# Splitting a two-layer product: full squares of the first two chunks on ScalarE, high and low matmuls in groups, later range checks, a third room for sums

## Chip, cores and metric

One NeuronCore of a Trainium2 chip. The metric is the device time of one execution, in microseconds; lower is better. The kernel before took 662.72 us (median of 3 runs, 662.3 to 664.31).

## What is computed

Attention with four sink columns and a window of 128, followed by two dense layers with a squared ReLU between them:

```python
keep = is_sink | in_window                      # 4 batches, 8 heads, 768 rows, 64 columns a head
a = softmax(where(keep, q @ k.T / 8, -1e9))
x = (a @ v), heads side by side                 # 3072 x 512
h = maximum(x @ w_in, 0)                        # 512 -> 2048
out = (h * h) @ w_out                           # 2048 -> 512
```

All of it is float32, and the result must be near float32.

## The kernel before

**Tiling.** The 3072 rows are eight chunks `c` of 384 (`TOK`). The 2048 hidden columns are 16 blocks `fc` of 128; one block of one chunk is called a column here, so there are 128 columns. The attention of a chunk (four pairs of heads) has to be done before its first column.

**A column.** Every operand is split into a high part (float32r, 4 bytes) and two float16 parts, the rounded high part and the rest. A product is then three matmuls: high by high, and two low ones with float16 weights. `first` (L1024) makes a column's hidden block: for each of four slices `cc` of the 512 inputs one high and two low matmuls, 12 in all, 384 columns wide, into one PSUM bank. The slices alternate, high-low-low and low-low-high. Then ScalarE makes `r`, the scaled ReLU (L1037), and its square `gh`, rounded to float32r (L1042). VectorE makes the square again at full precision in the bank (L1049) and subtracts `gh` from it (L1061), which is the low part `gc`; a cast (L511, L514) makes the float16 copy of `gh`. One column later `second` (L1084) multiplies these by the block of `w_out`: three groups `t` of 128 rows, each one high and two low matmuls, 512 wide, alternating in the same way, summed over all 16 blocks in three banks.

**Legs.** The columns are run in nine legs: the first 8 blocks of chunk 0, all 16 of chunk 1, the last 8 of chunk 0, then chunks 2 to 7. While the first two chunks run, the 32 rows of weights are still being loaded and split: ScalarE makes the high part (L427), VectorE puts the words together (L392, L399, L406) and makes the rest (L432). The attention of chunk 2 also lies there. `evacuate` (L1112) copies the three sums out at the end of a leg, into rooms `ob0`, `ob1` and, from chunk 2 on, `f2`; in the second leg of chunk 0 it first loads the part sums back.

**Range checks.** `scale_steps` (L479, 16 reductions of the split weights) are handed out with the columns of leg 3, which is chunk 2. `check_steps` and `value_steps` follow from leg 4. `verdict` (L1217) reduces all tables to a flag in one block of VectorE instructions six columns before the end.

**Order.** Nothing is scheduled at run time. `Plan` (L90) holds all steps with an engine or several, a cost, a rank, what they read and write, and which bank they take. `order` (L137) simulates the engines with these costs and writes each engine's instructions out in the order it finds: of the steps that can start soonest it takes the lowest rank, and a step with several engines goes to the one that ends first, plus a penalty in the fourth place. So a changed cost or choice moves instructions of all engines, far from the line that was changed.

Of the kernel before, what the change touches and what calls it, by code (L numbers as in the profile page):

```python
# [8 lines left out]
F32 = mybir.dt.float32  # L9
# [15 lines left out]
TOK = 384  # L25
NQ = TOK // P
WR = 512
BIG = 3.0e38
LIM = 5.0e8
W_LOW = 2.0**-22  # L30
W_HIGH = 2.0**33
# [29 lines left out]
TURNED = 2  # L61
# [3 lines left out]
CHECK = 4  # L65
# [3 lines left out]
G16_DVE = 0.2  # L69

# [135 lines left out]
def sink_window_attention_moe(  # L206
# [25 lines left out]
    with ExitStack() as fast:  # L232
# [139 lines left out]
        def bank(key):  # L372
            return banks[plan.got[key]]
# [631 lines left out]
        def products(c, f0, f1, item, checks):  # L1005
            xh, xc = xs[slot[c]]
            last = c == NCHUNK - 1
            pend = None
            for fc in range(f0, f1 + 1):
                n = item + fc - f0  # L1010
                if fc < f1:
# [5 lines left out]
                    for cc in range(NCC):  # L1017

                        def first(cc=cc, fc=fc, key=key):
                            wh, wc = wi[fc]()  # L1020
                            cols = slice(cc * P, (cc + 1) * P)
                            terms = ((wh, xh[:, cc]), (wc[:, 1], xc[:, 0, cc]), (wc[:, 0], xc[:, 1, cc]))
                            for j, (wt, xt) in enumerate(terms[:: -1 if cc % 2 else 1]):
                                nc.tensor.matmul(  # L1024
                                    bank(key)[:, 0:TOK], wt[:, cols], xt,
                                    start=(cc == 0 and j == 0), stop=(cc == NCC - 1 and j == 2),
                                )

                        add(
                            ("PE", 0.5, 0), n + 0.1 * cc, first,  # L1030
                            reads=[(t, slot[c], cc) for t in ("xh", "x16", "xl")] + [(t, 2 * fc) for t in ("w", "w16", "wl")]
                            + [(key, cc - 1)] * (cc > 0),
                            writes=[(key, cc)] + [("tick", n), "column"] * (cc == 0), take=[("h", key)] if cc == 0 else [],
                        )
# [3 lines left out]
                        reads=[(key, cc) for cc in range(NCC)], writes=["r"],  # L1038
# [13 lines left out]
                        reads=["r"], writes=[(key, cc) for cc in range(NCC)],  # L1052
# [16 lines left out]
                if pend:  # L1069
                    f, g, gh, gc = pend  # L1070
                    for t in range(NQ):
# [33 lines left out]

        def scaled(e, dst, src):
            if e == "ACT":
                nc.scalar.activation(dst, src, AF.Copy, scale=SUM_SCALE)
            else:
                nc.vector.tensor_scalar(dst, src, SUM_SCALE, None, op0=ALU.mult)  # L1110

        def evacuate(c, f0, f1, t, okey, n):  # L1112
# [3 lines left out]
            third = c >= 2  # L1116
# [100 lines left out]
        def verdict():  # L1217
            t = const.tile([P, 16], F32, name="checks")

            par = made["par"] = const.tile([P, 2], F32, name="par")  # L1220
# [5 lines left out]
            flat = vmax.rearrange("p a b -> p (a b)")  # L1226
            for x, (table, limit) in enumerate(
                (
                    (most[:, NCHUNK : NCHUNK + 2], LIM),
                    (wchk[:, 0, :], W_HIGH),  # L1230
                    (wchk[:, 1, :], 0.0),
                    (wmax, WS_MAX),
                    (flat, V_MAX),
                )
            ):
                at = x if x < 3 else x + 5
                nc.vector.tensor_reduce(t[:, at : at + 1], table, axis=AX.X, op=ALU.max)
                nc.vector.tensor_scalar(t[:, at : at + 1], t[:, at : at + 1], limit, None, op0=ALU.is_le)
            for at, table, limit in ((10, wmax, WS_MIN), (11, flat, V_MIN)):
                nc.vector.tensor_reduce(t[:, at : at + 1], table, axis=AX.X, op=ALU.min)  # L1240
                nc.vector.tensor_scalar(t[:, at : at + 1], t[:, at : at + 1], limit, None, op0=ALU.is_ge)
# [4 lines left out]
            made["good"] = const.tile([P, 1], F32, name="good")  # L1246
            nc.vector.tensor_reduce(made["good"], t[:, 0:12], axis=AX.X, op=ALU.min)
            made["ones"] = const.tile([P, 1], F32, name="ones")
            nc.vector.memset(made["ones"], 1.0)

# [10 lines left out]
        add(  # L1261
            ("DVE", 4.0), END, verdict,
            reads=["wchk", "wmax", "vmax", ("most", NCHUNK), ("most", NCHUNK + 1)],
            writes=["good"],
        )
# [242 lines left out]
```

## Time and profile before

| | |
|---|---|
| median of 3 runs | 662.72 us |
| the profiled execution | 662.91 us |
| its span, first to last instruction | 661.1 us |
| PE busy (matmul) | 643.0 us, 97% of the span |
| DVE, ACT, POOL busy | 485.2, 441.8, 183.3 us |
| mean granted TensorE clock | 0.996 |

PE is TensorE's matmul queue, PEld its weight loads, DVE VectorE, ACT ScalarE, POOL GpSimd. Matmuls overlap, so the start of one row may lie before the end of the row ahead of it; the distance from end to end is what a matmul costs in a dense stream. A busy PE is therefore not yet a PE at its peak.

### The profile page before, as it was taken

The page shows a single profiled execution, that of the slowest core. Times are in us where ns is not written, and L with a number is a line of the kernel's source. Part 1 is how long each engine was busy: PE and PEld are TensorE (multiplying, and loading weights), DVE is VectorE, ACT ScalarE, POOL GpSimd, SP SyncE. Part 2 cuts the span into 40 slices and gives each one's busy share as a digit, 9 for nine tenths or more (in the row PEclk, how much of TensorE's full clock was granted, in tenths as well). Part 3 has the DMA queues.
Part 4 walks back from the last instruction along what each step waited for, and adds up shares of the span by engine and source line. Part 5 has one row for each costly group of instructions (what it writes and reads, how often), then busy time and mean ns, then how long its engine had stood idle before and what let it go on. Part 6 is the DMA issues. An engine that isn't in the chain of part 4 may idle for free.

```text
span 661.1 us, 12158 instructions
## 1 busy us (share of the span) xinstructions
PE 643.0 (97%) x3734; PEld 405.8 (61%) x3734; DVE 485.2 (73%) x1328; ACT 441.8 (67%) x1358; POOL 183.3 (28%) x381
## 2 busy tenths in 40 slices
PE   8899999996999999999999999999999999999995
PEld 6665666663566566666666666666666665556663
DVE  8999999999778888776877867575767664343432
ACT  7998777765465565565578777777777785655421
POOL 4433414435223333332423122242322211000000
PEclk9999999998999999999999999999999999999999
DMA  8635554784745534455777767657667754322001
GB/s 289 246 128 182 168 196 122 219 239 115 198 136 165 156 109 128 126 165 152 182 200 213 218 202 193 174 166 202 173 175 220 219 173 141 124 88 72 17 1 53
DMA packets 85748, 106.54 MB, mean 161 GB/s; under 512 B 12760, under 2 KB 60376, under 8 KB 85676
## 3 DMA queue, kind: packets, MB, share of 16 engines
q1 hardware_dynamic: 85068, 105.05, 54.7%
q8 instruction: 31, 0.51, 0.3%
q10 hardware_dynamic: 576, 0.60, 0.3%
q14 instruction: 41, 0.34, 0.2%
q0 software_dynamic: 32, 0.05, 0.0%
HBM read 80.29 MB, written 24.38 MB: 158 GB/s over the span
## 4 chain that ended last, share of the span: by engine, by line
PE 88%; DVE 6%; DMA 2%; ACT 2%; issue 1%; POOL 0%; SPq 0%; DVEq 0%; ACTq 0%
PE bank L1024 37%; PE bank L1084 37%; PE bank L941 5%; PE bank L668 5%; PE bank L662 1%; DVE P L718 1%; PE bank L947 1%; DVE P L645 1%; DMA out_dram<-ob 1%; ACT P L651 1%; DMA sk<-SKT 1%; DVE wc L432 0%; DVE f L406 0%; DMA qn<-in_q_dram 0%; DVE f L399 0%
## 5 line engine op out<-in xcount | busy, mean ns | idle before, releaser
L1024 PE MATMUL bank<-xc,wc 128*128 128x384 f16 x1024 | 217.5, 329 | 0.5 <-DVE wc L432 0.5
L1084 PE MATMUL bank<-wc,gc 128*128 128x512 f16 (+1 forms) x800 | 215.1, 376 | 0.9 <-POOL gc L514 0.7
L1024 PE MATMUL bank<-xh,wh 128*128 128x384 f32 x512 | 198.8, 428 | 1.1 <-DVE gc L1061 0.6
L1084 PE MATMUL bank<-wh,gh 128*128 128x512 f32 (+1 forms) x400 | 166.9, 457 | 2.2 <-ACT gh L1042 1.6
L1037 ACT ACTIVATE r<-bank 128x384 f32<-128x384 f32 x128 | 62.6, 489 | 117.9 <-PE bank L1024 112.3
L1049 DVE SCALAR_TENSOR_TENSOR bank<-bank,r 128x384 f32<-128x384 f32 x128 | 72.0, 563 | 86.6 <-ACT r L1037 85.6
L718 POOL TENSOR_SCALAR P<-P,small 128x260 f32<-128x260 f32 (+1 forms) x164 | 87.1, 545 | 158.4 <-DVE small L711 150.5
L651 ACT ACTIVATE P<-P,nbs 128x260 f32<-128x260 f32 (+1 forms) x192 | 93.4, 487 | 43.8 <-DVE nbs L645 41.6
L1024 PEld LDWEIGHTS <-wc 128*128 128x128 f16 x1024 | 77.1, 98 | 70.0 <-issue 31.1
L1024 PEld LDWEIGHTS bank<-xh,wh 128*128 128x128 f32 x512 | 93.8, 190 | 25.6 <-DVE nbs L645 0.9
L1084 PEld LDWEIGHTS <-gc 128*128 128x128 f16 x800 | 56.1, 98 | 86.4 <-issue 48.8
L1084 PEld LDWEIGHTS bank<-wh,gh 128*128 128x128 f32 x400 | 76.2, 190 | 22.4 <-ACT gh L1042 2.1
L645 DVE CUSTOM_DVE_ANT_0 P<-bank,maskA 128x260 f32<-128x260 f32 x128 | 52.7, 420 | 30.7 <-PE bank L668 30.0
L668 PE MATMUL bank<-KS,QS 128*128 128x260 f32 (+1 forms) x288 | 69.0, 325 | 3.2 <-DVE nbs L645 2.4
L1061 DVE TENSOR_TENSOR gc<-bank,gh 128x384 f16<-128x384 f32 x128 | 70.1, 548 | 0.4
L1042 ACT ACTIVATE gh<-r 128x384 fp32r<-128x384 f32 x128 | 66.6, 520 | 3.0
L668 PEld LDWEIGHTS bank<-KS,QS 128*128 128x128 f32 x288 | 52.2, 190 | 14.3 <-DVE nbs L645 2.7
L877 DVE STREAM_TRANSPOSE T<-P 128x384 f32<-128x384 f32 x96 | 46.7, 495 | 1.0 <-POOL P L718 0.9
L625 POOL TENSOR_TENSOR KS<-kn,KS 128x396 fp32r<-128x396 f32 (+1 forms) x20 | 25.9, 1297 | 68.2 <-ACT KS L511 34.2
L941 PE MATMUL bank<-PT,vn 128*64 128x256 f32 (+1 forms) x392 | 37.0, 338 | 0.4 <-DVE xc L962 0.4
L651 ACT ACTIVATION_READ_ACCUMULATOR P<-P,nbs 128x1 f32 x192 | 36.0, 187 | 0.0
L511 DVE CAST gc<-gh 128x384 f16<-128x384 f32 x74 | 27.6, 373 | 10.4 <-ACT gh L1042 7.5
(129 smaller groups left out, 748.8 us busy)
## 6 DMA issues: line engine op xcount, KB each, us to landing
raw<-in_moe_w_dram SPq DMA_DIRECT2D x32, 512.0 KB, 3.7
half<-in_moe_w_dram SPq DMA_DIRECT2D x64, 256.0 KB, 2.9
via<-T SPq DMA_DIRECT2D x96, 96.0 KB, 2.0
PT<-via SPq DMA_DIRECT2D x24, 384.0 KB, 3.8
via<-T SPq DMA_DIRECT2D x96, 80.0 KB, 2.1
PT<-via SPq DMA_DIRECT2D x24, 320.0 KB, 3.9
kn<-in_k_dram SPq DMA_DIRECT2D x28, 264.0 KB, 4.3
qn<-in_q_dram SPq DMA_DIRECT2D x31, 192.0 KB, 3.6
```

The source lines that it names most:

```text
L645: nc.vector.tensor_tensor_reduce(Pt(h)[:, i, o : o + n], ps_[:, 0:n], mask[:, 0:n], -SCALE, BIG, ALU.add, ALU.min, nb)
L651: nc.scalar.activation(Pt(h)[:, i, o : o + n], Pt(h)[:, i, o : o + n], AF.Exp, bias=nb, scale=-1.0, accum_out=sm[:, h, i : i + 1],)
L668: nc.tensor.matmul(bank(key)[:, 0:n], QS(h)[:, cols], flat[:, a, c0 : c0 + n], start=(a == 0), stop=(a == 1),)
L718: {"POOL": nc.gpsimd, "DVE": nc.vector}[engine].tensor_scalar(a, a, rs[:, h, i : i + 1], 1.0, op0=ALU.mult, op1=ALU.mult)
L877: nc.vector.transpose(dst.rearrange("p c j b -> p j c b"), src.rearrange("p j (c b) -> p j c b", b=32))
L941: nc.tensor.matmul(xo[h * D : h * D + D, qs[0] * P : qs[0] * P + len(qs) * P], vn[:, kk, h, :], rhs(), start=(n == 0), stop=False, skip_gr ...
L1024: nc.tensor.matmul(bank(key)[:, 0:TOK], wt[:, cols], xt, start=(cc == 0 and j == 0), stop=(cc == NCC - 1 and j == 2),)
L1037: lambda key=key, r=r: nc.scalar.activation(r(), bank(key)[:, 0:TOK], AF.Relu, scale=R_SCALE),
L1042: lambda gh=gh, r=r, fc=fc: nc.scalar.activation(gh(), r(), AF.Square, accum_out=gsum[:, c % 2, fc : fc + 1]),
L1049: lambda key=key, r=r: nc.vector.scalar_tensor_tensor(bank(key)[:, 0:TOK], bank(key)[:, 0:TOK], R_SCALE, r(), op0=ALU.mult, op1=ALU.mult),
L1061: lambda key=key, gh=gh, gc=gc: nc.vector.tensor_tensor(gc()[:, 1], bank(key)[:, 0:TOK], f32(gh()), op=ALU.subtract),
L1084: nc.tensor.matmul(bank(okey)[:, cols], gt, wt[:, cols], start=(f == f0 and j == 0), stop=(f == f1 - 1 and j == 2),)
```

## The change

Four things are done:

1. The full square may go to ScalarE (`full_square`, as Square of `r` into the bank) or to VectorE. In the first two chunks VectorE carries a penalty of 3.0 us in the choice, from chunk 2 on none is set.
2. From chunk 2 on (`together`) a column's `first` is two steps: all 8 low matmuls, then all 4 high ones. In chunks 2 to 6, for the blocks but the last, `second` is two steps: the 3 high ones of all three sums, then the 6 low ones; the three banks are taken at once.
3. The weight reductions move from leg 3 to the last leg but one (chunk 6). The verdict is cut into small steps and starts a column earlier.
4. The second leg of chunk 0 uses the third room as well.

```diff
-                    for cc in range(NCC):
-                        def first(cc=cc, fc=fc, key=key):
...
+                    every = tuple(range(NCC))
+                    low_first = [(cc, x) for cc in every for x in (2, 1)]
+                    if together:
+                        runs = [low_first, [(cc, 0) for cc in every]]
+                    else:
+                        runs = [[(cc, x) for x in ((2, 1, 0) if cc % 2 else (0, 1, 2))] for cc in every]
+                    for m, run in enumerate(runs):
+                        def first(m=m, run=run, fc=fc, key=key, runs=runs):
+                            wh, wc = wi[fc]()
+                            for j, (cc, x) in enumerate(run):
...
-                        ("DVE", 0.47), n - 9,
-                        lambda key=key, r=r: nc.vector.scalar_tensor_tensor(
-                            bank(key)[:, 0:TOK], bank(key)[:, 0:TOK], R_SCALE, r(), op0=ALU.mult, op1=ALU.mult
-                        ),
+                        [("DVE", 0.47, "", 0.0 if together else FULL_DVE), ("ACT", 0.45)], n - 9,
+                        lambda e, key=key, r=r: full_square(e, bank(key)[:, 0:TOK], r()),
...
+                    if together and not last and f < f1 - 1:
+                        okeys = [("o", c, f0, t) for t in range(NQ)]
+                        def second_of(x, f=f, gh=gh, gc=gc, okeys=okeys):
+                            wh, wc = wo[f]()
+                            for t, okey in enumerate(okeys):
+                                ts_ = slice(t * P, (t + 1) * P)
+                                terms = ((gh()[:, ts_], wh), (gc()[:, 0, ts_], wc[:, 1]), (gc()[:, 1, ts_], wc[:, 0]))
+                                for j, (gt, wt) in enumerate(terms[1:] if x else terms[:1]):
...
+        def full_square(e, full, r):
+            if e == "ACT":
+                nc.scalar.activation(full, r, AF.Square)
+            else:
+                nc.vector.scalar_tensor_tensor(full, full, R_SCALE, r, op0=ALU.mult, op1=ALU.mult)
...
-            third = c >= 2
+            third = c >= TURNED or f0 > 0
...
-            for fc in range(f0, f1) if g == CHECK - 1 else ():
-                own[fc] = [scales.pop(0)]
             for fc in range(f0, f1) if g >= CHECK else ():
                 own[fc] = [checks.pop(0) for _ in range(min(1, len(checks)))]
+                if g == len(legs) - 2:
+                    own[fc].append(scales.pop(0))
...
-        END = item - 6
-        add(
-            ("DVE", 4.0), END, verdict,
...
+        END = item - 7
+        add(("DVE", 0.7), END, numbers, reads=[], writes=["checks"])
...
+            add(
+                ("DVE", 0.4), END, lambda at=at, table=table, limit=limit, op=op, is_=is_: within(at, table, limit, op, is_),
+                reads=reads + ["checks"], writes=[("checks", at)],
+            )
```

Three places show what the new order does. Line numbers of the rows after are those of the changed file: L1031 and L1086 are `first` and the new `second`, L1045, L1050, L1133 and L1067 the ReLU, `gh`, the full square on ScalarE and the low part; the weight lines are one higher than before.

ScalarE in chunk 1, two columns in a row, before (`wh` and `wc` are weights being split, `gc` the float16 copy of `gh`):

```order
L1037 ACTIVATE r_601<-bank_71 128x384
L1042 ACTIVATE gh_632,gsum<-r_601 128x384
L511 CAST gc_636<-gh_632 128x384
L427 ACTIVATE wh_1157<-f_1155 128x512
L511 CAST wc_1167<-wh_1157 128x512
L1037 ACTIVATE r_601<-bank_70 128x384
L1042 ACTIVATE gh_610,gsum<-r_601 128x384
```

and after, two columns of the first chunks:

```order
L1045 ACTIVATE r_592<-bank_70 128x384
L1050 ACTIVATE gh_630,gsum<-r_592 128x384
L1133 ACTIVATE bank_70<-r_592 128x384
L1045 ACTIVATE r_592<-bank_71 128x384
L428 ACTIVATE wh_1185<-f_1189 128x512
L1133 ACTIVATE bank_71<-r_592 128x384
```

Each column has a third ACTIVATE, the square into the bank, and the two casts that stood between the columns have gone to GpSimd. All 32 squares of the first two chunks stand on ScalarE and none of the other 96. Over the whole program ScalarE has 14 casts of `gh`, 9 of weights and 6 of `x` fewer, and 5 copies of K; GpSimd has 13, 7 and 6 of the casts more and 7 subtractions of K fewer; VectorE has 7 subtractions and 5 copies of K, 2 weight casts and 1 cast of `gh` more.

VectorE late in chunk 1, before, a piece of the 27 rows that stand between the low parts of the 21st and the 22nd column (`f` and `raw` are weight words, `T` turned probabilities of chunk 2):

```order
L406 SCALAR_TENSOR_TENSOR f_1782<-raw_1631,f_1782 128x512
L392 TENSOR_SCALAR f_1821<-raw_1651 128x512
L392 TENSOR_SCALAR f_1826<-raw_1722 128x512
L399 SCALAR_TENSOR_TENSOR f_1821<-raw_1651,f_1821 128x512
L711 RECIPROCAL small<-small 128x3
L877 STREAM_TRANSPOSE T_1_1851<-P_1_1707 128x3x4x32
L432 SCALAR_TENSOR_TENSOR wc_1799<-f_1782,wh_1785 128x512
L877 STREAM_TRANSPOSE T_1_1851<-P_1_1707 128x2x4x32
L406 SCALAR_TENSOR_TENSOR f_1821<-raw_1651,f_1821 128x512
L399 SCALAR_TENSOR_TENSOR f_1826<-raw_1722,f_1826 128x512
```

and after, the first 9 of the 11 rows that stand there now:

```order
L878 STREAM_TRANSPOSE T_0_1813<-P_0_1628 128x3x4x32
L433 SCALAR_TENSOR_TENSOR wc_1820<-f_1719,wh_1763 128x512
L878 STREAM_TRANSPOSE T_0_1813<-P_0_1628 128x2x4x32
L393 TENSOR_SCALAR f_1831<-raw_1641 128x512
L393 TENSOR_SCALAR f_1839<-raw_1713 128x512
L433 SCALAR_TENSOR_TENSOR wc_1820<-f_1775,wh_1763 128x512
L646 ISA P_0_1852,nbs<-bank_68,mask_97 128x128
L646 ISA nbs 128x1
L794 STREAM_TRANSPOSE SKT<-PSK 128x64
```

Before the low part of the 21st column 27 weight rows have been begun in the old order and 30 in the new one, out of 32: the weights have moved ahead, and less is left between the later columns.

PE in chunk 2, inside a `second`, where the second sum (bank 72) is closed and the third (bank 73) begins, before:

```order
L1084 MATMUL bank_72<-wc_1898,gc_628 128x512
L1084 MATMUL bank_72<-wh_1872,gh_610 128x512
L1084 MATMUL bank_73<-wh_1872,gh_610 128x512
L1084 LDWEIGHTS gc_628
L1084 MATMUL bank_73<-wc_1898,gc_628 128x512
```

and after, from the end of a `first` into the `second` behind it (bank 67 holds scores of the next chunk's attention):

```order
L1031 MATMUL bank_71<-xh_161,wh_776 128x384 x4
L1086 MATMUL bank_72<-wh_676,gh_630 128x512
L1086 MATMUL bank_74<-wh_676,gh_630 128x512
L1086 MATMUL bank_73<-wh_676,gh_630 128x512
L669 MATMUL bank_67<-KS_0_5086,QS_0_5097 128x128 x2
L1086 LDWEIGHTS gc_641
L1086 MATMUL bank_72<-wc_683,gc_641 128x512
```

The high matmuls of two sums stood in pairs, two and two. Now the four of `first` stand together, the three of `second` follow them directly, and its six low ones come behind those, followed by the eight low ones of the next `first`.

## Rows read from the trace of the kernel before

**Rows 1.** The page: the chain that ended last, shares of the span by engine.
```profile
PE 88%; DVE 6%; DMA 2%; ACT 2%; issue 1%; POOL 0%; SPq 0%; DVEq 0%; ACTq 0%
```

**Rows 2.** Windows: stretch, length, busy us of each engine (instructions), PE clock, DMA.
```profile
0.00:60.00 60.00, 55.52 (x356) 37.80 (x357) 58.22 (x195) 51.93 (x162) 24.20 (x62) 1.00 0.65 217
60.00:140.00 80.00, 80.00 (x461) 50.23 (x458) 78.05 (x189) 61.53 (x165) 28.69 (x53) 1.00 0.58 179
140.00:183.00 43.00, 36.68 (x204) 21.56 (x203) 35.63 (x89) 24.54 (x67) 18.71 (x28) 0.96 0.66 182
183.00:640.00 457.00, 456.25 (x2637) 287.20 (x2636) 307.12 (x841) 299.90 (x957) 111.66 (x238) 1.00 0.55 154
510.00:590.00 80.00, 80.00 (x460) 48.80 (x459) 42.63 (x115) 53.49 (x175) 11.71 (x28) 1.00 0.49 143
620.00:640.00 20.00, 20.00 (x120) 12.91 (x118) 9.24 (x35) 6.05 (x16) 0.00 (x0) 1.00 0.01 1
```

**Rows 3.** Waits of PE, 0 to 183 us: total us, times, longest.
```profile
PE bank L668 <- DVE nbs L645: 2.4, 1, 2.4
PE bank L1084 <- ACT gh L1042: 1.6, 1, 1.6
```

**Rows 4.** Timeline of DVE, 85 to 170 us: start, length; the low parts alone.
```profile
141.01 0.52 DVE L1061 TENSOR_TENSOR gc<-bank,gh 128x384 f16<-128x384 f32 x1
152.64 0.55 DVE L1061 TENSOR_TENSOR gc<-bank,gh 128x384 f16<-128x384 f32 x1
160.72 0.56 DVE L1061 TENSOR_TENSOR gc<-bank,gh 128x384 f16<-128x384 f32 x1
```

**Rows 5.** Groups by line and shape, whole span: busy us, mean ns | idle before, releasers.
```profile
L1049 DVE SCALAR_TENSOR_TENSOR bank<-bank,r 128x384 f32<-128x384 f32 x128 | 72.0, 563 | 86.6 <-ACT r L1037 85.6
L1061 DVE TENSOR_TENSOR gc<-bank,gh 128x384 f16<-128x384 f32 x128 | 70.1, 548 | 0.4
L1042 ACT ACTIVATE gh<-r 128x384 fp32r<-128x384 f32 x128 | 66.6, 520 | 3.0
L1037 ACT ACTIVATE r<-bank 128x384 f32<-128x384 f32 x128 | 62.6, 489 | 117.9 <-PE bank L1024 112.3 <-issue 5.0 <-DVE small L711 0.2
L625 DVE TENSOR_TENSOR KS<-kn,KS 128x396 fp32r<-128x396 f32 x13 | 7.7, 590 | 0.3
L625 POOL TENSOR_TENSOR KS<-kn,KS 128x396 fp32r<-128x396 f32 (+1 forms) x20 | 25.9, 1297 | 68.2 <-ACT KS L511 34.2
L511 DVE CAST gc<-gh 128x384 f16<-128x384 f32 x74 | 27.6, 373 | 10.4 <-ACT gh L1042 7.5
L511 ACT CAST gc<-gh 128x384 f16<-128x384 f32 x34 | 17.4, 511 | 1.0
L514 POOL CAST gc<-gh 128x384 f16<-128x384 f32 x20 | 13.4, 670 | 52.6 <-ACT gh L1042 52.6
L479 DVE TENSOR_REDUCE wmax<-wh 128x2 bf16<-128x1024 f32 x16 | 19.3, 1203 | 0.0
```

**Rows 6.** The chain in order of time, 491 to 500 us: start, us, what.
```profile
492.22 2.03 PE bank L1024 x12
494.25 2.03 PE bank L1084 x9
```

**Rows 7.** Timeline of PE, 491 to 495 us: three runs of one column's first product.
```profile
492.24 0.82 PE L1024 MATMUL bank<-xc,wc 128*128 128x384 f16 x4
492.76 0.65 PE L1024 MATMUL bank<-xh,wh 128*128 128x384 f32 x2
493.25 0.82 PE L1024 MATMUL bank<-xc,wc 128*128 128x384 f16 x4
```

**Rows 8.** Groups on PE and PEld by shape: the low first product, and a score's weight loads.
```profile
L1024 PE MATMUL bank<-xc,wc 128*128 128x384 f16 x1024 | 217.5, 329 | 0.5 <-DVE wc L432 0.5
L668 PEld LDWEIGHTS bank<-KS,QS 128*128 128x128 f32 x288 | 52.2, 190 | 14.3 <-DVE nbs L645 2.7 <-DVE QS L636 1.4
```

**Rows 9.** Timeline of PE, 168 to 169.3 us: four float32r score matmuls in a row.
```profile
168.53 0.64 PE L668 MATMUL bank<-KS,QS 128*128 128x260 f32 x4
```

More of the change, by code (lines that the diff above doesn't have):

```diff
@@ L69 @@
 G16_DVE = 0.2
+FULL_DVE = 3.0
 X_SCALE = 2.0**12
@@ L1006, in products @@
             xh, xc = xs[slot[c]]
-            last = c == NCHUNK - 1
+            last, together = c == NCHUNK - 1, c >= TURNED
             pend = None
@@ L1024, in first @@
                                 nc.tensor.matmul(
                                     bank(key)[:, 0:TOK], wt[:, cols], xt,
-                                    start=(cc == 0 and j == 0), stop=(cc == NCC - 1 and j == 2),
+                                    start=(m == 0 and j == 0), stop=(m == len(runs) - 1 and j == len(run) - 1),
                                 )
-                        add(
[L1030 to L1033, printed above, removed]
+                        names = sorted({(("xh", "x16", "xl")[x], cc) for cc, x in run})
@@ new lines, in products @@
+                        weights = [(t, 2 * fc) for t in (("w", "w16", "wl") if not together else ("w16", "wl") if m == 0 else ("w",))]
+                        add(
+                            ("PE", sum(0.163 if x else 0.175 for _, x in run), 0), n + 0.4 * m / len(runs), first,
+                            reads=[(t, slot[c], cc) for t, cc in names] + weights + [(key, m - 1)] * (m > 0),
+                            writes=[(key, m)] + [("tick", n), "column"] * (m == 0), take=[("h", key)] if m == 0 else [],
@@ L1037, in products @@
                         lambda key=key, r=r: nc.scalar.activation(r(), bank(key)[:, 0:TOK], AF.Relu, scale=R_SCALE),
-                        reads=[(key, cc) for cc in range(NCC)], writes=["r"],
+                        reads=[(key, m) for m in range(len(runs))], writes=["r"],
                     )
@@ L1047, in products @@
                     add(
[L1048 to L1052 removed]
+                        [("DVE", 0.47, "", 0.0 if together else FULL_DVE), ("ACT", 0.45)], n - 9,
+                        lambda e, key=key, r=r: full_square(e, bank(key)[:, 0:TOK], r()),
+                        reads=["r"], writes=[(key, m) for m in range(len(runs))],
                     )
@@ L1070, in products @@
                     f, g, gh, gc = pend
-                    for t in range(NQ):
+                    if together and not last and f < f1 - 1:
[6 more added lines that the diff above has]
+                                for j, (gt, wt) in enumerate(terms[1:] if x else terms[:1]):
+                                    nc.tensor.matmul(
+                                        bank(okey)[:, 0:DM], gt, wt, start=(f == f0 and x == 0), stop=False,
+                                    )
+                        for x in range(2):
+                            add(
+                                ("PE", 1.296 if x else 0.696, 0), n + 0.5 + 0.2 * x, lambda x=x, second_of=second_of: second_of(x),
+                                reads=[("g16", g), ("gl", g), ("w16", 2 * f + 1), ("wl", 2 * f + 1)] if x else [("gh", g), ("w", 2 * f + 1)],
+                                writes=okeys, take=[("o", okey) for okey in okeys] if f == f0 and x == 0 else [],
+                            )
+                    for t in range(0 if together and not last and f < f1 - 1 else NQ):
                         okey = ("o", c, f0, t)
@@ L1215, in sink_window_attention_moe, with within, numbers @@
                     )
-        def verdict():
-            t = const.tile([P, 16], F32, name="checks")
+        def within(at, table, limit, op=ALU.max, is_=ALU.is_le):
+            t = made["checks"]
+            nc.vector.tensor_reduce(t[:, at : at + 1], table, axis=AX.X, op=op)
+            nc.vector.tensor_scalar(t[:, at : at + 1], t[:, at : at + 1], limit, None, op0=is_)
+        def numbers():
+            made["checks"] = t = const.tile([P, 16], F32, name="checks")
             par = made["par"] = const.tile([P, 2], F32, name="par")
@@ L1225, in verdict, with limits @@
             nc.vector.tensor_tensor(t[:, 6:8], par, low, op=ALU.is_equal)
[L1226 to L1241, printed above, removed]
+        def limits():
+            t = made["checks"]
             nc.vector.tensor_scalar(t[:, 3:4], ns, float(NS), None, op0=ALU.is_le)
```

30 lines of the change are left out of this document (22 added, 8 removed).

## The prediction

> **What bounds the kernel now.** I read the page's chain first, then busy time by windows, then the waits in the one stretch that stands out. The chain gives PE 88% and no other engine over 6% [rows 1]. So the end is set by the number of matmuls and their spacing, except where PE runs dry, and the windows say where [rows 2]. From 60 to 140 us PE is busy 80.00 of 80, from 183 to 640 us 456.25 of 457. From 140 to 183 us it is busy only 36.68 of 43: 6.32 us idle, and the mean granted clock is 0.96, which is below the upper of its two levels (1.2 and 2.4 GHz) after the engine had stood idle. Read as 0.04 of 43 us, that is another 1.7 us. About 8.0 us are lost there. From 0 to 60 us PE is idle for 4.5 us, but there VectorE is busy 58.22 of 60 and the inputs are only arriving.
>
> Who makes PE wait at 140? The releasers name VectorE and ScalarE, 2.4 and 1.6 us in the two longest waits [rows 3], but ScalarE is busy only 24.54 of the 43 us and VectorE 35.63 [rows 2], so I look at VectorE's work for a column. The low parts of three columns in a row start at 141.01, 152.64 and 160.72 us [rows 4], 11.6 and 8.1 us apart, while a column of two products costs PE 2.03 + 2.03 = 4.06 us [rows 6]. Each low part is queued behind what VectorE's order has put ahead of it: 27 rows of weights and attention between the first two, of which the order above shows a piece. In the stretch before, VectorE was busy 78.05 of 80 us [rows 2]: it had kept up with PE only by pushing weight rows back, and this is where they come due.
>
> **1. Full squares to ScalarE.** VectorE loses 32 squares of 0.563 = 18.0 us [rows 5]. It takes over 7 subtractions of K at 0.590 = 4.1 us and 8 casts and copies at 0.373 = 3.0 us (5 K, 2 weights, 1 `gh`; the widths differ a little, an estimate by the cast's row) [rows 5]. Net 10.9 us less in about 180, more than the 8.0 lost. The order agrees: 11 rows in place of 27 stand between those two low parts, and 30 weight rows in place of 27 are begun before the first of them. At the mean of the 27 rows, 11.6 / 27 = 0.43 us, 11 rows are 4.7 us, about one column.
>
> Who pays? ScalarE gets 32 squares. No row shows ScalarE writing a bank; the nearest are `r`, which reads one, at 0.489, and `gh` at 0.520 [rows 5]. I take 0.489 since it has one PSUM side too and no sum beside it: 15.6 us. It gives up 14 + 9 + 6 casts and 5 copies, 34 of about 0.511 = 17.4 us [rows 5]. Even. GpSimd gets 26 casts at 0.670 = 17.4 us and loses 7 subtractions at 1.297 = 9.1 us [rows 5]: 8.3 us more, on an engine that is busy 71.6 of the first 183 us [rows 2]. The float16 copy of `gh` is later on GpSimd by 0.670 - 0.511 = 0.16 us, plus any queue.
>
> A column's own chain grows: `r` and `gh`, then the square behind `gh` on the same engine, then the low part: 0.489 + 0.520 + 0.489 + 0.548 = 2.05 us. Before, VectorE's square ran beside `gh`: 0.489 + 0.563 + 0.548 = 1.60. One column of PE work, 4.06 us, lies between a first product and the second that needs it, or at least its 2.03 us of other work; I book nothing, and what queueing would do is a rival below.
>
> Of the 8.0 us I take 7.5, since a little of the clock loss may stay. Bounds: 0, if something else is just as late, and 9.7, the 8.0 with the clock's 1.7 once more, for matmuls that are shown as busy but stretched by what they wait for.
>
> **2. Matmuls in groups.** In one column the ends of three runs lie at 493.06, 493.41 and 494.07 us [rows 7]: two highs cost 0.35 (0.175 each), four lows behind a high 0.66. Within a run the lows are (0.82 - 0.329) / 3 = 0.164 apart [rows 7, 8]. In one run of eight and one of four the column is 8 x 0.164 + 4 x 0.175 = 2.01 against 2.03 [rows 6]: -0.02 x 96 columns = -1.9. For `second` half of that, as its highs already stand two and two: -0.01 x 75 = -0.75. The rows are rounded to 0.01, so the sum of -2.6 is soft: I take -2.5, with bounds of twice the saving, -4.9, and of +0.01 a column, +1.0.
>
> Does a row of highs wait for its weights? A float32r load takes 190 ns [rows 8], longer than the 175 of the matmul above it. But four float32r score matmuls in a row take 0.64 us from the first start to the last end; one alone takes some 0.28, an estimate from the 329 ns of 384 columns less 124 columns at 2.4 GHz. So they are (0.64 - 0.28) / 3 = 0.12 us apart, with 190-ns loads [rows 8, 9]. Loads overlap each other there, so they do not set the spacing; I book nothing. The Trainium skill (TensorE: Matmul & The Clock Gate, section "Weight-path perf modes — Fast Weight Load (FWL) and DoubleRow") says that float32 weights get no fast load, and its section "Back-to-back issue gap" that spacing is set by load and matmul both; by these the runs of highs would be bound by their loads, a rival below.
>
> The three banks of a leg's sums are now taken at once. Between a leg's last sum and the next leg's first `second` lies a `first` of 2.03 us [rows 6], and the copies out, of the size of a bank-reading `r` (0.489 each) [rows 5], go to two engines. Cost 0; at most 0.5 us at five legs, 2.5, if a copy is late.
>
> **3. Scales, verdict, room.** The 16 reductions are 16 x 1.203 = 19.3 us of VectorE [rows 5], moved to chunk 6. There VectorE is busy 42.63 of 80 us while PE is busy 80.00 [rows 2], so both the move and the load are hidden: 0 in the new place. The verdict's steps, near 620 us, lie where VectorE is busy 9.24 of 20 and PE 20.00 of 20 [rows 2]: 0 as a block, 0 in pieces. In the stretch after 183 us PE idles 0.75 us in all [rows 2]; freed of scales and given a third room, I take 0.7 of it as gone; at worst none is.
>
> **4. Start.** The order of the first 60 us changes as well, with VectorE's squares of eight columns gone while it is busy 58.22 of 60 [rows 2]. That could help, or another load order could hurt: 0, with 2 us either way.
>
> **Sum.** The profiled execution took 662.91 us, 0.19 above the median of 662.72. 662.9 - 7.5 - 2.5 - 0.7 = 652.2; against the median **652.0 us**.
>
> **Rivals.**
> *The wait only moves.* ScalarE, GpSimd or the weights' DMA is just as late as VectorE was. For it: the casts of `gh` go to the slowest engine for them, 0.670 [rows 5]; DMA is at 0.66 in the stretch [rows 2]. Against it: none of them is busy more than 0.66 of 140 to 183 us, and PE's long waits name only VectorE and ScalarE [rows 2, 3]. Then only 0.7 and 2.5 stay: 659.5 us.
>
> *The loads bound the runs of highs.* A `first` with four highs would cost 8 x 0.164 + 0.174 + 3 x 0.190 = 2.056 us, with the 190 of [rows 8], +0.03 on 2.03 at most; less some 0.01 of the switch saved, +0.018 x 96 = +1.7, and -0.7 for `second` beside it: +1.0 in place of -2.5, so 655.5 us. Against it [rows 9].
>
> *Slower: ScalarE's chain comes onto PE's path.* Three ACTIVATEs of each of 32 columns now stand one behind the other, among weights and exponentials. It decides once the queueing on ScalarE passes 4.06 - 2.05 = 2.0 us a column. Then each column waits for at least the added square: 32 x 0.489 = 15.6 us, with nothing won at 140: 662.7 + 15.6 - 2.5 - 0.7 = 675 us. For it: ScalarE is busy 61.53 of 80 us from 60 to 140, and some 18 squares make it 70 if the casts did not leave. Against: they do leave, in the order.
>
> That the change does not do what it says is ruled out by the order: all 32 squares stand on ScalarE.
>
> **How the numbers follow.** Forecast 0.72, with a range of its own from 662.7 - 9.7 - 4.9 - 0.7 = 647.5 to 656, where half of the stall's gain is missing; wait moves 0.13; loads bind 0.10; slower 0.05. The range of 8 in 10 reaches from 647.5 to the first rival's 659.5. A measurement of this kernel tells 0.3%, 2.0 us, from no change: slower has the last rival's 0.05, same 0.06 (the first rival with a late bank or a poor start added), faster 0.89.
>
> **What would show it.** Right: in 140 to 183 us PE busy above 42 of 43, its clock at 1.00, low parts some 4 us apart; ScalarE's square at 0.45 to 0.55 us; `first` at about 2.01 in the chain; VectorE busier by some 19 us in chunk 6 with PE still full. Wrong: PE's waits there name the square on ScalarE, GpSimd's cast or a `raw` load; highs in runs 0.19 apart; idle PE at the legs' starts, waiting for a bank; or a stall of the same size elsewhere before chunk 3.

## The result and the profile after

The changed kernel took **653.28 us** (median of 4 runs, 652.44 to 653.33) against 662.73 (662.3 to 664.31) of the kernel before beside it: a ratio of 0.985, with a 95% interval of 0.9832 to 0.9868. That is 9.45 us faster; 10.7 were forecast.

The place the forecast was made for first. Windows of the changed kernel (stretch, length, busy us of each engine with its instructions, PE clock, DMA), where [rows 2] has those of before:

```profile
0.00:60.00 60.00, 52.84 (x342) 36.93 (x343) 57.16 (x198) 49.60 (x155) 26.48 (x58) 0.94 0.61 202
60.00:140.00 80.00, 78.92 (x450) 48.57 (x447) 78.71 (x182) 60.22 (x165) 40.56 (x63) 1.00 0.64 192
140.00:183.00 43.00, 42.50 (x242) 26.29 (x241) 35.78 (x97) 30.86 (x91) 18.26 (x33) 1.00 0.66 175
183.00:630.00 447.00, 447.00 (x2619) 300.15 (x2618) 304.46 (x823) 291.44 (x943) 110.67 (x240) 1.00 0.57 158
500.00:580.00 80.00, 80.00 (x466) 52.67 (x465) 61.05 (x144) 51.11 (x172) 18.15 (x38) 1.00 0.52 149
```

From 140 to 183 us PE is busy 42.50 of 43 where it was 36.68, and its clock is 1.00 where it was 0.96. From 183 to 630 us PE is never idle. In chunk 6 VectorE is busy 61.05 of 80 (from 500 to 580 us, as the columns come some 10 us earlier now), 18.4 more than in [rows 2], with PE still full: there are the scales. But the start is worse than before: PE 52.84 of 60 in place of 55.52, and from 60 to 140 us PE is idle 1.1 us where it was never idle. The clock of 0.94 in place of 1.00 says less than it seems to, since the record of before begins late; the last section comes back to it.

The waits of PE from 0 to 183 us, the longest (total us, times, longest), against [rows 3]:

```profile
PE bank L777 <- POOL PSK_wide L730: 1.7, 2, 1.5
PE bank L663 <- DVE nbs L646: 1.4, 2, 1.1
```

The 2.4 and 1.6 us of before are gone. Two waits are new. `nbs` is the first chunk's row maxima, in the first 10 us. `PSK_wide` holds sink probabilities that GpSimd makes, and its long wait comes later (timeline of PE: start, length, what, the idle time before it in brackets):

```profile
43.33 0.55 PE L777 MATMUL bank<-ident,PSK_wide 128*128 128x128 f32 x3 [1.50 <-POOL PSK_wide L730]
```

The groups that answer to [rows 5] and [rows 8] (busy us, mean ns | idle before):

```profile
L1031 PE MATMUL bank<-xc,wc 128*128 128x384 f16 x1024 | 196.2, 327 | 0.0
L1133 ACT ACTIVATE bank<-r 128x384 f32<-128x384 f32 x32 | 15.3, 477 | 0.0
L515 POOL CAST gc<-gh 128x384 f16<-128x384 f32 x33 | 21.6, 656 | 65.0 <-ACT gh L1050 64.7
```

ScalarE's square takes 477 ns; 489 were taken for it. It never waits, since it stands behind `gh` on its own engine.

The chain in order of time, 482 to 489 us (start, us, what), and the timeline of PE there, against [rows 6] and [rows 7]:

```profile
482.25 1.99 PE bank L1086 x9
484.25 2.00 PE bank L1031 x12
486.24 2.01 PE bank L1086 x9
```

```profile
482.78 1.47 PE L1086 MATMUL bank<-wc,gc 128*128 128x512 f16 x6
484.08 1.46 PE L1031 MATMUL bank<-xc,wc 128*128 128x384 f16 x8
485.25 0.99 PE L1031 MATMUL bank<-xh,wh 128*128 128x384 f32 x4
486.08 0.86 PE L1086 MATMUL bank<-wh,gh 128*128 128x512 f32 x3
```

A column costs 2.00 + 2.00 us in place of 2.03 + 2.03. The four highs of `first` end 486.24 - 485.54 = 0.70 us after the lows, 0.175 each: their loads of 190 ns do not set the spacing.

So two terms gave what was expected or more, and something at the start took part of it back. The first product of the 21st column ended 4.95 us *later* than in the kernel before (143.73 in place of 138.78), that of the 24th 5.6 us earlier. VectorE's timeline shows what is new in the first 10 us (start, length, instruction):

```profile
6.36 0.16 DVE L1257 TENSOR_SCALAR par<-parf 128x2 f32<-128x2 f32 x1
...
6.76 0.51 DVE L1259 SCALAR_TENSOR_TENSOR par<-parf,par 128x2 f32<-128x2 f32 x1
...
7.43 0.43 DVE L646 CUSTOM_DVE_ANT_0 P<-bank,mask 128x260 f32<-128x260 f32 x1
...
8.26 1.14 DVE L1266 TENSOR_TENSOR checks<-parf 128x1 f32<-128x1 f32 x1
...
9.55 0.43 DVE L646 CUSTOM_DVE_ANT_0 P<-bank,maskA 128x260 f32<-128x260 f32 x1
```

The lines from 1257 on are the verdict. Cut into steps, two of them (`numbers` and `limits`, nine instructions) read nothing but the parameters, so they are ready from the start, and the planner sets by earliest start before rank: it put the last check of the program among the first chunk's row maxima. They take VectorE from 6.36 to 7.43 and from 8.13 to 9.55 us, 2.5 us in all. PE waits right behind:

```profile
10.04 2.70 PE L663 MATMUL bank<-kn,qn 64*128 64x128 f32 x12 [1.07 <-DVE nbs L646]
```

and after that idle time its granted clock falls to the lower level, from 11.2 to 18.0 us by the trace's clock record (windows as above):

```profile
8.00:12.00 4.00, 2.93 (x15) 2.36 (x16) 3.96 (x22) 2.98 (x13) 1.29 (x2) 0.90 0.90 332
12.00:16.00 4.00, 3.62 (x17) 2.89 (x16) 3.97 (x21) 3.59 (x14) 1.60 (x6) 0.50 1.04 379
```

In the expectations below, "PE's loss" of a stretch is its length less the sum of its matmuls, each at the median distance of ends that its kind has in the dense stretches of the kernel before. It is 8.6 us from 0 to 60 and 10.0 from 140 to 183 us in the kernel before, 11.8 and 0.7 in the changed one.

### The profile page after: what moved, and what is told of

Read it like the earlier page. It is cut to its first block, busy times and chain, and to the rows that moved or that the text cites. A ratio compares the mean times of both kernels' runs of the same rounds, so it can differ in the third digit from the quotient of the medians.

```text
span 651.6 us, 12170 instructions
## 1 busy us (share of the span) xinstructions
PE 636.4 (98%) x3736; PEld 421.9 (65%) x3736; DVE 482.9 (74%) x1315; ACT 436.0 (67%) x1361; POOL 196.0 (30%) x391
## 4 chain that ended last, share of the span: by engine, by line
PE 81%; DVE 14%; issue 2%; ACT 1%; POOL 0%; DVEq 0%; POOLq 0%; ACTq 0%
PE bank L1031 34%; PE bank L1086 23%; PE bank L1109 11%; PE bank L942 5%; PE bank L669 5%; DVE f L407 2%; DVE P L646 2%; DVE wc L433 2%; DVE f L400 2%; PE bank L948 1%; DVE f L393 1%; DVE gc L1067 1%; PE bank L663 1%; DVE P L719 1%; PE bank L849 1%
## 5 line engine op out<-in xcount | busy, mean ns | idle before, releaser
L1031 PE MATMUL bank<-xc,wc 128*128 128x384 f16 x1024 | 196.2, 327 | 0.0
L1031 PE MATMUL bank<-xh,wh 128*128 128x384 f32 x512 | 146.6, 386 | 0.0
L1045 ACT ACTIVATE r<-bank 128x384 f32<-128x384 f32 x128 | 62.6, 489 | 115.0 <-PE bank L1031 90.2
L1031 PEld LDWEIGHTS <-wc 128*128 128x128 f16 x1024 | 90.7, 98 | 66.7 <-issue 9.2
L1086 PE MATMUL bank<-wc,gc 128*128 128x512 f16 x450 | 110.2, 381 | 0.0
L1135 DVE SCALAR_TENSOR_TENSOR bank<-bank,r 128x384 f32<-128x384 f32 x96 | 54.1, 563 | 63.7 <-ACT r L1045 63.4
L1031 PEld LDWEIGHTS bank<-xh,wh 128*128 128x128 f32 x512 | 90.9, 189 | 13.1 <-ACT P L652 0.3
L1109 PE MATMUL bank<-wc,gc 128*128 128x512 f16 (+1 forms) x350 | 90.8, 364 | 0.4 <-DVE gc L1067 0.4
L1086 PEld LDWEIGHTS <-gc 128*128 128x128 f16 x450 | 38.0, 98 | 52.9 <-issue 9.1
L1109 PE MATMUL bank<-wh,gh 128*128 128x512 f32 (+1 forms) x175 | 71.4, 445 | 0.2 <-DVE ob L1141 0.2
L1067 DVE TENSOR_TENSOR gc<-bank,gh 128x384 f16<-128x384 f32 x128 | 70.1, 548 | 0.7 <-ACT bank L1133 0.3
L1050 ACT ACTIVATE gh<-r 128x384 fp32r<-128x384 f32 x128 | 66.5, 520 | 3.2
L1086 PE MATMUL bank<-wh,gh 128*128 128x512 f32 x225 | 64.8, 396 | 0.0
L515 POOL CAST gc<-gh 128x384 f16<-128x384 f32 x33 | 21.6, 656 | 65.0 <-ACT gh L1050 64.7
L1086 PEld LDWEIGHTS bank<-wh,gh 128*128 128x128 f32 x225 | 38.8, 188 | 3.2
```

Source lines behind the costliest of these rows:

```text
L1031: nc.tensor.matmul(bank(key)[:, 0:TOK], wt[:, cols], xt, start=(m == 0 and j == 0), stop=(m == len(runs) - 1 and j == len(run) - 1),)
L1045: lambda key=key, r=r: nc.scalar.activation(r(), bank(key)[:, 0:TOK], AF.Relu, scale=R_SCALE),
L1050: lambda gh=gh, r=r, fc=fc: nc.scalar.activation(gh(), r(), AF.Square, accum_out=gsum[:, c % 2, fc : fc + 1]),
L1067: lambda key=key, gh=gh, gc=gc: nc.vector.tensor_tensor(gc()[:, 1], bank(key)[:, 0:TOK], f32(gh()), op=ALU.subtract),
L1086: nc.tensor.matmul(bank(okey)[:, 0:DM], gt, wt, start=(f == f0 and x == 0), stop=False,)
L1109: nc.tensor.matmul(bank(okey)[:, cols], gt, wt[:, cols], start=(f == f0 and j == 0), stop=(f == f1 - 1 and j == 2),)
```

## Experiments

All ran with 4 or 5 timed runs beside the kernel before, whose median was 663.18 us beside experiments 1 to 4, 662.38 beside 5 to 8 and 662.97 beside 9 and 10 (662.73 beside the changed kernel above). These groups ran on three chips, so a difference between experiments of two groups is sure to some 0.8 us only. The theory: the squares take the stall away, the groups give the rest, and the early verdict takes some 3 us back. The rivals: the start is covered by VectorE's later queue; the stall would move; the loads bound the highs.

### 1. The nine instructions late, all else in its place

```diff
 def numbers():
-    made["checks"] = t = const.tile([P, 16], F32, name="checks")
-    par = ...
+    made["checks"] = const.tile([P, 16], F32, name="checks")
...
 def verdict():
+    late()        # the bodies of numbers() and limits()
```

> The changed kernel with one edit: the nine small VectorE instructions of the verdict that need only the parameters (at 6.36 to 9.55 us in the trace of the changed kernel) are written out at the end of the verdict; every other instruction keeps its place on every engine. Theory A (they hold up the start: 2.5 us of VectorE ahead of the first row maxima, PE idle for 1.07 us, its granted clock at 0.5 to 0.9 from 8 to 20 us, and nothing gives that back later): PE's loss from 0 to 60 us falls from 11.8 towards the 8.6 of the kernel before, so 650.1 us (649.5 to 651.0). Rival B (VectorE is full until 140 us anyway, so the start is made up for there): 653.3 us, within 1. Rival C (the order was planned with these instructions in it, so the rest of the start doesn't use the time): 652 us.

Measured 651.07 us (650.91 to 651.19), ratio 0.9821 (0.9807 to 0.9834). The start, by windows:

```profile
8.00:12.00 4.00, 3.98 (x26) 3.01 (x23) 3.92 (x24) 4.00 (x20) 2.43 (x6) 1.00 0.94 326
12.00:16.00 4.00, 3.82 (x32) 3.05 (x32) 3.97 (x15) 4.00 (x15) 1.00 (x4) 1.00 1.03 378
40.00:60.00 20.00, 18.50 (x115) 10.94 (x115) 19.41 (x50) 17.63 (x49) 8.83 (x12) 1.00 0.46 154
```

The gap is gone, no fall of the clock is recorded from 8 to 20 us, and 2.2 us are won: theory A in kind, between A's 650.1 and C's 652 in size. B falls: nothing before 140 us makes the start up. From 40 to 60 us PE is still idle 1.5 us, where the kernel before was idle 0.18:

```profile
40.00:60.00 20.00, 19.82 (x124) 11.55 (x123) 19.92 (x51) 17.35 (x48) 6.64 (x12) 1.00 0.55 169
```

That part isn't the verdict's. It is there in every run with the squares on ScalarE, 1.2 us in experiment 2 and 1.3 in experiment 6, and PE is idle for 0.18 us again in experiment 5, which has them on VectorE.

### 2. The same, planned anew

```diff
-add(("DVE", 0.7), END, numbers, reads=[], writes=["checks"])
+add(("DVE", 0.7), END, numbers, reads=[("most", NCHUNK + 1)], writes=["checks"])
```

> The changed kernel with the same nine instructions tied in the plan to the last maximum of the row bounds, so that the whole order is planned anew without them at the start; up to PE's 138th row it is then the order of the kernel before. Theory A: 649 to 650.5 us, clock 1.00 from 8 to 20 us, the first product of the fourth column ends within 1 us of 56.6 us. Rival B (a start that is better goes into VectorE's queue before 140 us): 653.3 us. A third reading, that all of the 4.9 us by which the changed kernel is behind at the 21st column comes from the start: 648.4 us.

Measured 649.32 us (648.74 to 650.15), ratio 0.9798 (0.9784 to 0.9811): 4.0 us less than the changed kernel, 13.4 to 13.9 less than the kernel before, and the lowest median of all here. So the nine instructions cost 2.2 us by themselves and 1.8 more by the order that had been planned around them. The fourth column's first product ends at 57.15 us, 59.79 in the changed kernel and 56.64 in the kernel before. From 60 to 140 us PE's idle time is 0.25 us, no longer 1.1:

```profile
60.00:140.00 80.00, 79.75 (x457) 49.69 (x456) 77.83 (x190) 62.64 (x168) 39.79 (x58) 1.00 0.62 190
140.00:183.00 43.00, 42.78 (x253) 26.66 (x252) 34.66 (x91) 30.34 (x90) 17.10 (x32) 1.00 0.70 188
```

### 3. The clock alone

`WARM` is the stretch of the plan's time in which it fills a gap of PE with idle matmuls.

```diff
-WARM = (12.0, 24.0)
+WARM = (6.0, 24.0)
```

> The changed kernel with three idle matmuls (identity by identity, into a free bank) more on PE near 9 us, where it waits for VectorE; nothing else is moved. This tells the clock from the wait. Theory A1 (the lower clock costs part of the start's loss): granted clock 1.00 from 8 to 20 us and 651.0 to 652.0 us. Rival A2 (VectorE's 2.5 us alone set the start, PE's clock is hidden under them): 653.3 us, within 0.6.

Measured 652.75 us (652.6 to 653.29). No fall of the clock is recorded, and 0.5 us are won, within what A2 allows: VectorE sets the start, and PE's slower matmuls lie under it for the most part. The fall isn't even certain. Experiments 4, 7 and 9 have the same order at the start; the profiles of 4 and 7 record none, that of 9 one from 13.0 to 16.4 us.

### 4. Alternating matmuls inside the same steps

```diff
+mixed = [(a, b) for a in every for b in ((2, 1, 0) if a % 2 else (0, 1, 2))]
+if len(runs) == 2:
+    run = mixed[8:] if m else mixed[:8]
```

and in the same way for the nine of `second`, three in its first step and six in the other.

> The changed kernel with the matmuls inside each step in the old alternating order (high, low, low, low, low, high); the steps, their bounds and the places of all instructions of the other engines are the same. Theory (grouping is worth 0.02 us a column of first products and 0.01 of second ones): 653.3 + 2.5 = 655.8 us, and by the trace, where the stretches after 183 us run 2.3 us faster than the old spacing, 655.6; bounds 652.3 to 658.2. Rival (loads bound the runs of highs, grouping costs 1.0): 652.3 us.

Measured 656.88 us (656.71 to 656.99), ratio 0.9909 (0.9893 to 0.9924): the groups are worth 3.6 us. The rival falls; its sign is wrong. (By the columns' ends in the two profiles it is 3.8, from the 33rd column to the last.)

### 5. All squares on VectorE

```diff
-[("DVE", 0.47, "", 0.0 if together else FULL_DVE), ("ACT", 0.45)], n - 9,
+[("DVE", 0.47), ("DVE", 0.47)], n - 9,
```

on top of experiment 2.

> The kernel of e2 (nine verdict instructions late, 649.3 us) with all full squares on VectorE again; grouping, scales, verdict and room stay. VectorE's order is then that of the kernel before up to the 32nd column, with 27 rows between the 21st and 22nd low parts and 27 weight rows begun before. Theory (the stall of 140 to 183 us is VectorE's and the squares alone take it away): it comes back whole. PE's loss there, counted against its own dense spacing, is 10.0 us in the kernel before and 0.4 in e2, so 658.9 us (657.5 to 660.0); with the 7.5 of the prediction 656.8 us. Rival (the wait only moves, the stall was not VectorE's): 649 to 651 us.

Measured 658.58 us (657.89 to 658.8), 9.3 more than experiment 2. The stall is back, row for row [rows 2, 3, 4]. First the window, then PE's waits, then VectorE's timeline, the low parts alone:

```profile
140.00:183.00 43.00, 36.76 (x204) 21.71 (x203) 36.11 (x89) 24.70 (x69) 18.76 (x28) 0.96 0.70 186
```

```profile
PE bank L669 <- DVE nbs L646: 2.4, 1, 2.4
PE bank L1109 <- ACT gh L1050: 1.6, 1, 1.6
```

```profile
141.38 0.51 DVE L1067 TENSOR_TENSOR gc<-bank,gh 128x384 f16<-128x384 f32 x1
153.03 0.54 DVE L1067 TENSOR_TENSOR gc<-bank,gh 128x384 f16<-128x384 f32 x1
161.12 0.56 DVE L1067 TENSOR_TENSOR gc<-bank,gh 128x384 f16<-128x384 f32 x1
```

In the changed kernel those of the 20th to the 23rd column start 5.0, 4.5 and 7.2 us apart, closer than the 11.7 and 8.1 us here, but not the 4 us that the prediction wanted throughout:

```profile
142.12 0.55 DVE L1067 TENSOR_TENSOR gc<-bank,gh 128x384 f16<-128x384 f32 x1
147.09 0.56 DVE L1067 TENSOR_TENSOR gc<-bank,gh 128x384 f16<-128x384 f32 x1
151.63 0.54 DVE L1067 TENSOR_TENSOR gc<-bank,gh 128x384 f16<-128x384 f32 x1
158.88 0.55 DVE L1067 TENSOR_TENSOR gc<-bank,gh 128x384 f16<-128x384 f32 x1
```

### 6. The squares alone

The kernel before, with the choice of engine for the square and `full_square` of the change, and nothing else of it.

> The kernel before with the squares of the first two chunks offered to ScalarE under the same penalty, and nothing else of the change: alternating matmuls, scales in leg 3, verdict in one block, two rooms in the second leg of chunk 0. All 32 squares go to ScalarE. Theory (parts add up): 662.9 - 9.6 = 653.3 us (652.5 to 655), PE busy above 42 of 43 us from 140 to 183. Prediction's size of the term: 655.2 us. Rival (without the moved scales VectorE is late again in chunk 2): PE idle again between 183 and 240 us, 655 to 657 us.

Measured 654.92 us (654.21 to 655.34), 7.5 less than the kernel before beside it (662.38), ratio 0.9884 (0.9869 to 0.9899): at the upper end of the theory. From 140 to 183 us PE is full, so the stall went whole; and the 0.75 us of idle time after it is what it was before, so the rival's lateness did not grow:

```profile
140.00:183.00 43.00, 43.00 (x257) 27.00 (x255) 33.72 (x95) 29.53 (x89) 15.44 (x31) 1.00 0.65 172
183.00:240.00 57.00, 56.25 (x321) 35.30 (x321) 47.76 (x116) 36.48 (x104) 18.01 (x34) 1.00 0.53 147
```

So the squares are worth 7.5 us here and 9.3 between experiments 5 and 2. The traces settle most of the 1.8 between the two. This is by how much the first product of a column ends earlier than in the profile of the kernel before (us, less than zero is later):

| | 21st column | 33rd (chunk 2 begins) | last |
|---|---|---|---|
| changed kernel | -4.95 | 4.10 | 9.37 |
| experiment 2 | -1.21 | 8.22 | 13.49 |
| experiment 4, alternating | -4.56 | 4.47 | 5.97 |
| experiment 5, squares on VectorE | -0.37 | -0.20 | 5.06 |
| experiment 6, squares alone | -1.81 | 8.09 | 8.10 |

Experiments 2 and 5 are 8.4 us apart at the 33rd column and at the last; 0.8 of their 9.3 us comes behind the last column, and nearly half of that outside the profiled span. Experiment 6 has 8.1. The stall itself, from the 21st to the 33rd column, is worth 9.4 in experiment 2 and 9.9 in experiment 6, but both are later at the 21st column than the kernel before, by 1.2 and 1.8 us. The longest wait of PE from 40 to 60 us is for `PSK_wide` from GpSimd in both, 1.0 and 1.1 us; neither experiment 5 nor the kernel before has it there. That GpSimd's added casts make it late was not tried.

### 7. Alternating in the first product alone

Experiment 4's edit of `first`, without that of `second`.

> The changed kernel with the matmuls of the first product alone in the old alternating order, inside the same steps; the second product stays grouped. e4, with both alternating, took 656.88 us, 3.6 more than the changed kernel. If the gain follows the number of columns as predicted (0.02 of 96 first products, 0.01 of 75 second ones, so 1.9 of 2.6): 653.3 + 0.72 x 3.6 = 655.9 us. If only the first product gains: 656.9 us; if all of it is the second's: 653.3 us.

Measured 655.76 us (655.53 to 656.27): 2.5 of the 3.6 us are the first product's, 1.1 the second's, near the ratio of the prediction (1.9 to 0.75).

### 8. The scales back in chunk 2

```diff
-                if g == len(legs) - 2:
-                    own[fc].append(scales.pop(0))
+            for fc in range(f0, f1) if g == CHECK - 1 else ():
+                own[fc] = [scales.pop(0)]
```

on top of experiment 2.

> The kernel of e2 with the 16 scale reductions (19.3 us of VectorE) back in leg 3, chunk 2. Theory (both places are covered, since PE is full in both): 649.3 us, within 0.7. Rival (VectorE is late in chunk 2 with them, as the 0.75 us of idle PE of the kernel before between 183 and 240 us suggest): 650.0 to 651.0 us, with PE idle there.

Measured 649.51 us (648.88 to 650.02), within 0.2 of experiment 2, which is less than the two can be told apart. The rival falls: PE is full in chunk 2 with them; VectorE is busy 47.84 there and 41.46 without:

```profile
183.00:240.00 57.00, 57.00 (x331) 37.90 (x331) 47.84 (x118) 37.63 (x108) 17.44 (x35) 1.00 0.51 140
```

### 9. High, low, low, four times

Experiment 7 with `(0, 1, 2)` for every slice.

> The changed kernel with the first product's matmuls in the order high, low, low four times over, inside the same steps; the second product stays grouped. Inside a column that is seven changes between high and low, against four in e7 (655.76 us) and one in the changed kernel (653.28 us). Theory D (each change between kinds costs the same, (655.76 - 653.28) / (96 x 3) = 8.6 ns): 653.3 + 96 x 6 x 8.6 ns = 658.2 us (657.5 to 659). Rival E (it is the pairs of highs, whose loads don't overlap, that cost, and singles cost less): below 655.8 us.

Measured 658.35 us (658.08 to 659.16), where D gave 658.2. Theory E falls. But one, four and seven are the changes inside a column alone: a first product that begins with a high makes one more against the lows ahead of it, and one that ends with a low one more against the highs behind it. Counted over all matmuls in the traces of PE, the changed kernel has 651 changes, experiment 7 has 955, experiment 4 has 1131 and this one 1339 (the kernel before 1139). Against the changed kernel that is 2.48 us for 304, 3.60 for 480 and 5.07 for 688: 8.2, 7.5 and 7.4 ns for a change, whether the highs stand singly, in pairs or in fours. Changes up and down were not told apart. In the timeline of PE a lone high with its two lows takes 0.52 us (483.86 to 484.38, start to start of the lows):

```profile
483.86 0.50 PE L1034 MATMUL bank<-xc,wc 128*128 128x384 f16 x2
484.06 0.47 PE L1034 MATMUL bank<-xh,wh 128*128 128x384 f32 x1
484.38 0.50 PE L1034 MATMUL bank<-xc,wc 128*128 128x384 f16 x2
```

### 10. Two rooms in the second leg of chunk 0

```diff
-third = c >= TURNED or f0 > 0
+third = c >= TURNED
```

on top of experiment 2.

> The kernel of e2 with two rooms for sums in the second leg of chunk 0, as in the kernel before. Theory (the third room is what took the last 0.2 us wait for a sum after 183 us away, at most): 649.3 to 649.6 us. Rival (the loads of the part sums come later with two rooms, and the next leg's sums wait): 650 us or more, with PE waiting for a sum's copy between 180 and 240 us.

Measured 650.75 us (650.48 to 651.1), 1.4 more than experiment 2: the rival. PE's waits from 0 to 300 us have a new longest one, at the first `second` of chunk 2, for the copy of a sum:

```profile
PE bank L1086 <- DVE ob L1164: 1.7, 1, 1.7
```

The kernel before had two rooms and waited 0.2 us for a sum there. The grouped `second` takes its three banks at once, so the last copy out holds up all three: in the timeline the third high waits, and the six lows behind it with it. By this the third room pays for the groups; no run has the third room without them.

## Why the prediction was right, and where not

**What bounds it, and the squares: right.** The stall was VectorE's queue and went whole with 32 squares. Its term, 7.5 with bounds 0 and 9.7, measured 7.5 (experiment 6) and 9.3 (experiment 5), 8.1 and 8.4 by the columns' ends. That is net of the 1.2 to 1.8 us that experiments 2 and 6 lose ahead of the 21st column, which the prediction had not seen. PE's longest new wait there is for GpSimd, an engine that the rival "the wait only moves" named, but 100 us before the place it had in mind. The column's chain of 2.05 us leaves out the read of `gh`'s sum behind it (128 on ScalarE, 188 ns each), without consequence. That VectorE's relief of 10.9 us would do, that ScalarE stays even (60.22 of 80 us busy from 60 to 140, 61.53 before) and that GpSimd has room (40.56 of 80) all held.

**Groups: right, too small.** 2.5 was taken, 3.6 measured, inside the bounds. The step that was mis-sized is "2.01 against 2.03": row ends rounded to 0.01 can't give 0.026 us. Counted in changes of kind, 488 fewer than before at 7.4 to 8.2 ns, it is 3.6 to 4.0; but that price comes from the experiments. The rival of the loads fell: the highs in runs stand 0.175 us apart, under the 190 ns of a load, where it wanted 0.19.

**Scales, verdict, room: two terms wrong, each by its own step.** "The verdict's steps, near 620 us, lie where VectorE is busy 9.24 of 20" was the failed step: nine of their instructions don't lie there. The order shows them between VectorE's first row maxima; the prediction looked at it in chunks 1 and 2 alone, and never asked what holds a step back that reads nothing. They cost 4.0 us, 2.2 directly. The 0.7 for "freed of scales and given a third room" came, since PE's 0.75 us of idle time after 183 us is gone, but not by the scales: with them in their old place it stays away (experiment 8), and their move is worth nothing that the runs can tell. The third room is worth 1.4, and that beside the grouped `second`, where the prediction had booked 0 with 0.5 a leg for late copies. The 0.75 us is not the squares' either (experiment 5 is full from 183 to 240 us without them), nor the grouping's inside the steps (experiment 4 is full as well); that leaves the cut into steps and the third room, and between these it stays open.

**Start: outside its bound.** "0, with 2 us either way" met a loss of 4.0 us. The rival "the wait only moves" was partly true in a form it did not have: a new wait for VectorE, 130 us earlier. That the total came out within 1.3 us is in part luck: the loss was made up by terms that were taken too small. By the table in experiment 6 the squares gave 8.4 (experiment 2 less 5), the nine instructions took 4.1 by the 33rd column (2 less the changed kernel) and 0.2 was lost besides. From there to the last column alternating matmuls gain 1.5 (experiment 4), with the 0.75 us of idle time in it, and the groups 3.8 more: 8.4 - 4.1 - 0.2 + 1.5 + 3.8 = 9.4, the table's 9.37 against the measured 9.45.

**Slower rival.** ScalarE's queue did not decide. The largest part of its own waiting from 60 to 183 us is the other way round, 12.8 us in which `r` waits for the first product.

## What to carry to other kernels

When a block is cut into small steps for a scheduler, each piece takes only the dependencies that it names. A piece that needs nothing will be set at the very start, where every microsecond is on the path: look in the new order for where each piece went, and tie such pieces to something late. An engine's backlog that falls due late (VectorE 78 of 80 us busy, then 27 rows between two columns) is worth more than its share of busy time shows. And two parts of a change can hang together: beside the groups the third room was worth 1.4 us, where the kernel before, without them, waited 0.2 us for a sum.

## What the runs showed of the hardware

A change between float32r and float16 matmuls on PE costs about 8 ns: 651, 955, 1131 and 1339 changes in the traces, with 653.28, 655.76, 656.88 and 658.35 us.

Two of the nine instructions were far longer at the start than late in the program: the 128x1 maximum of line 1266 took 1136 ns there and 150 in experiment 2, the 128x2 product of line 1259 took 514 and 161. Both read two tensors from SBUF, and each ends with a GpSimd instruction that began before it (line 530 runs from 6.65 to 7.25 us, line 537 from 8.12 to 9.37):

```profile
6.65 0.60 POOL L530 CAST VS<-vs 24x512 fp32r<-24x512 f32 x1
8.12 1.25 POOL L537 TENSOR_TENSOR VS<-VS,vs 24x512 fp32r<-24x512 f32 x1
```

The Trainium skill (SBUF — State Buffer, section "SBUF: two separate sides") says that VectorE and GpSimd share a pair of SBUF ports as an exclusive lock, which an instruction of VectorE with two SBUF inputs takes against one of GpSimd that reads SBUF. These rows agree with it: by them some 1.3 us of the 2.5 are waiting for GpSimd, (1136 - 150) + (514 - 161) ns. In experiment 4 the same maximum starts later beside the same GpSimd instruction, takes 0.36 us, and ends with it again (9.34 and 9.32 us):

```profile
8.98 0.36 DVE L1269 TENSOR_TENSOR checks<-parf 128x1 f32<-128x1 f32 x1
8.06 1.26 POOL L537 TENSOR_TENSOR VS<-VS,vs 24x512 fp32r<-24x512 f32 x1
```

No run here moved the two GpSimd instructions away, so this was read and not tried.

The granted clock of the first microseconds has to be read beside the matmuls. The windows show 1.00 also for time ahead of the trace's first clock record, and that record is a rise to the upper level: at 4.38 us in the profile of the changed kernel, at 9.94 in experiment 4's, at 10.49 in that of the kernel before. The same score matmul took 637 ns in experiment 4 from 7.3 to 8 us and 431 on average from 10.8 to 12 us; in the changed kernel it took 380 already from 6.9 to 7.6 us (groups of PE in these three windows: busy us, mean ns | idle before):

```profile
L663 PE MATMUL bank<-kn,qn 64*128 64x260 f32 x4 | 1.1, 637 | 0.0
L663 PE MATMUL bank<-kn,qn 64*128 64x260 f32 x8 | 1.6, 431 | 0.0
L663 PE MATMUL bank<-kn,qn 64*128 64x260 f32 x4 | 0.6, 380 | 0.0
```

So the early ones of experiment 4, and of the kernel before, where it is 637 ns from 7.3 to 8 us too, ran at the lower level without a record of it. The 1.00 of [rows 2] for the first 60 us leaves that out, and the changed kernel's profile, which records a fall from 11.2 to 18.0 us, had the upper level some 6 us earlier than these two. What the fall costs is little: the fourth column's first product ends at 59.79 us in the changed kernel and at 59.69 in experiment 9, which record one, and at 59.41, 59.19 and 59.09 in experiments 4, 7 and 3, which record none and have the same order there (3 with its idle matmuls). That fits the 0.5 us of experiment 3.
